# A polysketch attention and routed-experts kernel: shorter float64 conversion, expert work from chunk 1 of batch 0 on, P's stores on one queue, VectorE's part of the evacuations one step later

## The chip, the cores and the metric

The kernel runs on one core of one Trainium2 chip. A core has five engines that run their own instruction queues and meet at semaphores: TensorE (PE: matmuls out of SBUF into PSUM, with weight loads, PEld, beside them), VectorE (DVE), ScalarE (ACT), GpSimd (POOL) and SyncE (SP, which here issues the DMAs). The metric is device microseconds of one execution, the median of several. The profile is of one execution of its own; its span runs from the first to the last instruction of the program.

## The reference

Two blocks in a row, all float32 but for S1 and S2, which arrive as float64.

```python
# attention: B, H, S, D = 4, 4, 1088, 32; r = 8
phi(x) = outer(S1 @ x, S2 @ x)            # 64 features of each row
kv = sum_s phi(k)[s] * v[s];  z = sum_s phi(k)[s]
attn = phi(q) @ kv / (phi(q) . z + 1e-6)
x = attn as rows of (B*S, H*D) = (4352, 128)
# routing: E = 8 experts, F = 1024
P = exp(x @ w_gate - max)
for _ in range(8):
    P /= P.sum(1) + 1e-9;  P /= P.sum(0) + 1e-9;  P *= N / E
out = sum_e P[:, e] * (relu(x @ w1[e]) @ w2[e])
```

So the experts' matrix products need x alone; only their weighting needs P, and P needs the logits of all 4352 rows.

## The kernel before, in words

**Attention.** Each batch goes in three chunks of columns (384, 352 and 352 of 1088). Per batch, `transpose_k` and `transpose_q` turn k and q on VectorE (L247, L249, L241), `keys_ab` projects the keys on TensorE (L260, L264) and ScalarE copies the result to `ab` (L262, L265), `keys_products` multiplies the features on VectorE in three parts (`kp`, L276), and `keys_sums` sums them over the rows on TensorE (L291) and copies the four blocks of the result to `kvz`, by turns on ScalarE (L302) and VectorE (L300). Per chunk, `query_products` (L316, with ScalarE's copies `qa` at L321), `multiply` (VectorE, L328), `fractions` (TensorE, numerator and denominator, L338) and `divide` (VectorE, L350 to L357, writes the columns of `xT`) follow each other. The chunks' query products need four PSUM banks: those of batch 0 are the four banks in which the experts' sums lie later, those of the other batches come from the pool `aps` of four, which the fractions, the key work and the experts' first products share.

**Expert work.** The rows are cut into five pairs of tiles, one pair of 256 columns each and four of 480 each. Six items of expert work (expert 0 on each of the five pairs, expert 1 on pair 1) need no P: they are "plain", their results are kept and weighted at the end. The other 34 items multiply x by a row of P first (`xe`, on GpSimd, L530). An item has four quads, and a quad `k` has four steps `c`. In a step, `first(k, c)` makes a hidden block (L676) and ScalarE takes its ReLU (L680); `combine(k - 1)` makes sums and differences of hidden blocks on VectorE, in step 0 one instruction (L686) and in step 1 two (L688, L689); `second` makes up to two of the seven products (L725) of the quad two before (`LAG = 2`), which are gathered in four PSUM banks. So the seven products per quad stand for eight, and the parts of the result have to be put together afterwards.

**Evacuation.** When the last quad of a group of items has been multiplied, `part(g, k)` takes one of its four banks per step: ScalarE copies (L609, L610, L618, L622 to L624, L629) and VectorE additions. `add_now` (L560) puts an addition at once in VectorE's queue, behind the copies it waits for; `add` (L557) puts it in the list `later`, from which one is taken per step.

**Order.** `steps()` is a generator of these steps, and `fill(n)` takes n units from it, where a step of a 480-column pair is one unit and one of the 256-column pair 256/480. The attention functions are called in an order written out by hand with `fill` between them; `manual_schedule` keeps that order on the engines named, and the other engines' order is made by a scheduler. For batch 0 VectorE, TensorE and ScalarE are ordered by hand, from batch 1 on VectorE and TensorE. Before the change the first `fill(1)` stands after the multiplication of batch 0's last chunk. The generator `attention(b)` yields twelve times per batch, and `counts` has the units between. `routing()` follows: the logits of the three chunks (L363), their transposes (L372) and maximum, the exponential on ScalarE (L448), and eight iterations, each with row sums, scaling and column sums on VectorE (`cs`, L454 to L460), a small matmul that adds the columns up (L464), and the scaling by columns (L467, L470). Between an iteration's `cs` and its matmul stand 3.75 units of expert work. Then `lgT` is turned (L474) and P is stored to DRAM as `pT`, a quarter per batch, by turns from the SyncE and the ScalarE queue (L476); GpSimd's first `xe` reads it back through a DMA. `fill(7)` follows, and the rest of the steps after it.

**Start.** S1 and S2 come as pairs of 32-bit words, and `f64_to_f32` (L33 to L50) makes float32 of them with 16 VectorE instructions on 128x64; L207 turns the result, and `wd` and `wq` are made of it. 17 matmuls on ones (L118) run meanwhile on TensorE.

Of the kernel before, what the change touches and what calls it, by code (L numbers as in the profile page):

```python
# [10 lines left out]
F32 = mybir.dt.float32  # L11
U32 = mybir.dt.uint32
Act = mybir.ActivationFunctionType
Alu = mybir.AluOpType
# [4 lines left out]
def f64_to_f32(nc, pool, raw, shape):  # L19


    p, n = shape
    low, high = raw[:, 0::2], raw[:, 1::2]

    def u32(name):
        return pool.tile([p, n], U32, name=name)

    def f32(name):
        return pool.tile([p, n], F32, name=name)

    mant, tail, top, expo, rest = u32("mant"), u32("tail"), u32("top"), u32("expo"), u32("rest")
    out, ef, inside, over = f32("s12"), f32("ef"), f32("inside"), f32("over")
    nc.vector.tensor_scalar(mant, high, 3, 0x3FFFFFF8, op0=Alu.logical_shift_left, op1=Alu.bitwise_and)  # L33
    nc.vector.tensor_scalar(tail, low, 29, None, op0=Alu.logical_shift_right)
    nc.vector.tensor_scalar(top, high, 0xC0000000, None, op0=Alu.bitwise_and)
    nc.vector.tensor_scalar(rest, low, 0x1FFFFFFF, None, op0=Alu.bitwise_and)
    nc.vector.tensor_tensor(mant, mant, tail, op=Alu.bitwise_or)
    nc.vector.tensor_scalar(expo, high, 20, 0x7FF, op0=Alu.logical_shift_right, op1=Alu.bitwise_and)
    nc.vector.tensor_copy(out, rest)
    nc.vector.tensor_tensor(mant, mant, top, op=Alu.bitwise_or)  # L40
    nc.vector.tensor_copy(ef, expo)

    nc.vector.tensor_scalar(top, mant, 0xFF800000, None, op0=Alu.bitwise_and)

    nc.vector.tensor_scalar(inside, ef, 896.5, None, op0=Alu.is_ge)
    nc.vector.tensor_scalar(over, ef, 1150.5, 3e38, op0=Alu.is_ge, op1=Alu.mult)
    nc.vector.scalar_tensor_tensor(out, out, 2.0 ** -52, top.bitcast(F32), op0=Alu.mult, op1=Alu.mult)
    nc.vector.tensor_tensor(inside, inside, over, op=Alu.add)
# [6 lines left out]
def kernel(  # L55
# [12 lines left out]
    nc = tc.nc  # L68
# [45 lines left out]
    ones = consts.tile([P, P], F32, name="ones")  # L114
    nc.gpsimd.memset(ones, 1.0)
    warm = aps.tile([P, 512], F32, tag="a", name="a")
    for _ in range(17):
        nc.tensor.matmul(warm[:, 0:P], ones, ones, start=True, stop=True)  # L118
    own = consts.tile([P, H], F32, name="own")
    nc.gpsimd.memset(own, 0.0)  # L120
# [27 lines left out]
    loaded = {}  # L148
# [86 lines left out]

        return bank() if b else mps.tile([P, 512], F32, tag=f"s{i}", name="s")

    def transpose_q(b):
        qx = loaded[b][1]
        qT = wk.tile([P, S], F32, tag="qT", name="qT")  # L240
        nc.vector.transpose(out=qT, in_=qx.rearrange("p a d -> p (a d)"))  # L241
        queries[b] = qT

    def transpose_k(b):
        kx = loaded[b][0]
# [35 lines left out]
    def keys_sums(b):  # L281

        kp, vx = products.pop(b), loaded[b][2]
        pv = bank()[:, 0:128].rearrange("p (i c d) -> p i c d", i=2, c=2)
        slots = (slice(0, 3, 2), slice(1, 3), slice(2, 4), slice(2, 5, 2))

        for t in range(NT + 1):
            n = P if t < NT else 64
            for h in range(H):
                i, s = divmod(h, 2)  # L290
                nc.tensor.matmul(pv[64 * s:64 * (s + 1), i], kp[0:n, H * t + h].rearrange("p i j -> p (i j)"),  # L291
                                 vx[0:n, slots[h], t, :], start=(t == 0 and i == 0), stop=(t == NT and i == 1),
                                 tile_position=(0, 64 * s))

        kvz = summed[b % 2]
        for i in range(2):
            for s in range(2):
                sl = slice(64 * s, 64 * (s + 1))
                if s:
                    nc.vector.tensor_copy(kvz[sl, :, i, s, :], pv[sl, i])  # L300
                else:
                    nc.scalar.copy(kvz[sl, :, i, s, :], pv[sl, i])  # L302
        keys[b] = kvz
# [70 lines left out]
    def attention(b):  # L374


        follows = b + 1 < B
        query_products(b, 0)
        yield
        keys_sums(b)  # L380
        if b + 2 < B:
            load_kq(b + 2)
            load_v(b + 2)
        multiply(b, 0)
        if follows:
            transpose_k(b + 1)
        yield
        fractions(b, 0)
        yield
        divide(b, 0)  # L390
        if follows:
            keys_ab(b + 1)
        yield
        query_products(b, 1)
        yield
        multiply(b, 1)
        if follows:
            transpose_q(b + 1)
        yield
        fractions(b, 1)  # L400
        yield
        divide(b, 1)
        if follows:
            keys_products(b + 1, 0)
        yield
        query_products(b, 2)
        yield
        multiply(b, 2)
        if follows:
# [19 lines left out]
    def routing():  # L429
# [70 lines left out]
    later = []  # L500

    def prepare_w(j):
        if j == 0:
# [42 lines left out]
    def part(g, k):  # L546
# [7 lines left out]
        def tile_(tag, pool=keep, bufs=1, width=NMAX):  # L554
            return pool.tile([P, width], F32, tag=tag, name=tag, bufs=bufs)[:, 0:n]

        def add(out, a, b):  # L557
            later.append(lambda: nc.vector.tensor_tensor(out, a, b, op=Alu.add))  # L558

        def add_now(out, a, b):  # L560
            nc.vector.tensor_tensor(out, a, b, op=Alu.add)  # L561

        def put(t):
            y = (y1, y2)[t]
# [69 lines left out]
        if all(own.get(x) for x in (0, 2, 3)) and "v" not in own:  # L634
            own["v"] = True
            add_now(w[upper], own["p7"][upper], own["r"][upper])
            add(z, z, w)
            add(y2, z, f)
            if weighted:
                later.append(lambda: put(1))  # L640
        if all(own.get(x) for x in range(4)):
            add(y1[upper], z[upper], m[upper])
            if weighted:
                later.append(lambda: put(0))

    ends = (nc.scalar, nc.sync, nc.gpsimd, nc.scalar), (nc.sync, nc.scalar, nc.gpsimd, nc.sync)

# [85 lines left out]
    def steps():  # L733

        combined = iter(())
        for k in range(len(quads) + LAG):
# [17 lines left out]
            for c in range(4):  # L754
                if k < len(quads):
                    first(k, c)
                if c == 0 and 0 < k <= len(quads):
                    combined = combine(k - 1)
                next(combined, None)
                for p in todo[2 * c:2 * c + 2]:  # L760
                    second(*p)
                share = pair(groups[items[quads[min(k, len(quads) - 1)][0]][0]][0])[1] / NMAX
                if k >= len(quads):
                    while later:
                        later.pop(0)()
                elif later and (c % 2 or share > 0.9):
                    later.pop(0)()
                yield share
# [50 lines left out]
    with tc.manual_schedule(engines={engines.DVE, engines.PE}):  # L819
# [41 lines left out]
```

## Time and profile before

The median is 964.56 us (3 runs, 964.4 to 964.95). The profiled execution has a span of 962.4 us.

| what | before |
|---|---|
| TensorE busy | 945.7 us, 98% of the span |
| VectorE busy | 559.8 us, 58% |
| ScalarE busy | 393.8 us, 41% |
| GpSimd busy | 121.9 us, 13% |
| granted TensorE clock | 0.997 |
| L676, first expert products | 2560 instructions |
| L725, second expert products | 2240 instructions |
| DMA | 82.34 MB, mean 86 GB/s |

How to read it: a float32 matmul of the program stands as two instructions, and matmuls overlap, so a busy TensorE is not one that works at its full pace. The pace is better read from the number of instructions that start in a stretch. VectorE's share of 58% is a mean of two different stages: in the first 200 us, with the attention and the routing, it is 69 to 95% busy in most stretches of 10 us, and afterwards about 50%. A wait of VectorE or ScalarE matters only where TensorE comes to wait for its result.

### The profile page before, as it was taken

What the parts mean: (1) busy time and instruction counts of PE and PEld (TensorE: products, weight loads), DVE (VectorE), ACT (ScalarE), POOL (GpSimd) and SP (SyncE); (2) the same over time, 40 slices, a digit from 0 to 9 for tenths busy, and PEclk for the clock granted to TensorE, in tenths of its full rate; (3) what the DMA queues carried; (4) which work ended last, traced back from release to release, by engine and by line L of the source; (5) the groups of instructions that cost most, each with busy time, mean ns of one, the idle gap of its engine ahead of it and who ended that gap; (6) DMA issues with size and microseconds to landing.
All of it is one profiled execution on the core that took longest, in us unless ns stands there. A gap on an engine that the chain in (4) does not pass through costs nothing.

```text
span 962.4 us, 13494 instructions
## 1 busy us (share of the span) xinstructions
PE 945.7 (98%) x5510; PEld 393.4 (41%) x5510; DVE 559.8 (58%) x767; ACT 393.8 (41%) x754; POOL 121.9 (13%) x105
## 2 busy tenths in 40 slices
PE   8999999999999999999999999999999999999996
PEld 6644434333333333433333333333333333346664
DVE  7777669875555556844445644444574444447555
ACT  2344344454333334433334433333443333345443
POOL 1000000040222222300002000000200000011100
PEclk9999999999999999999999999999999999999998
DMA  6500000132222222522222422222242222236430
GB/s 191 180 23 1 2 1 1 47 124 62 86 86 84 86 85 96 135 86 85 87 85 95 119 87 86 86 86 86 88 126 86 87 77 78 77 89 167 148 111 12
DMA packets 75405, 82.34 MB, mean 86 GB/s; under 512 B 22416, under 2 KB 60304, under 8 KB 75344
## 3 DMA queue, kind: packets, MB, share of 16 engines
q1 hardware_dynamic: 74288, 81.22, 27.7%
q8 instruction: 43, 0.70, 0.3%
q10 hardware_dynamic: 992, 0.20, 0.1%
q0 software_dynamic: 64, 0.07, 0.1%
q14 instruction: 18, 0.15, 0.0%
HBM read 75.44 MB, written 6.04 MB: 85 GB/s over the span
## 4 chain that ended last, share of the span: by engine, by line
PE 85%; DVE 3%; ACT 1%; issue 0%; POOL 0%; POOLq 0%; DVEq 0%; ACTq 0%
PE a L676 44%; PE s L725 39%; PE a L338 0%; DVE t L686 0%; PE a L316 0%; DVE t L689 0%; DVE cs L460 0%; DVE t L688 0%; DVE y L558 0%; DVE w L561 0%; PE a L291 0%; DVE z L561 0%; PE a L363 0%; DVE rs L454 0%; DVE z L558 0%
## 5 line engine op out<-in xcount | busy, mean ns | idle before, releaser
L676 PE MATMUL a<-xe,w 128*64 128x480 f32 (+1 forms) x2176 | 629.8, 528 | 0.0
L680 ACT ACTIVATE h<-a 128x480 f32<-128x480 f32 (+1 forms) x640 | 341.3, 534 | 517.7 <-PE a L676 505.0
L725 PE MATMUL s<-t,ws 128*64 128x480 f32 (+1 forms) x960 | 416.6, 529 | 0.4 <-DVE t L688 0.3
L686 DVE TENSOR_TENSOR t<-h 128x960 f32<-128x960 f32 (+1 forms) x160 | 215.7, 1349 | 344.4 <-ACT h L680 344.4
L676 PEld LDWEIGHTS a<-xe,w 128*64 128x64 f32 x2176 | 226.8, 137 | 239.6 <-issue 222.4
L725 PE MATMUL s<-h,w 128*64 128x480 f32 (+1 forms) x640 | 286.0, 529 | 0.0
L725 PEld LDWEIGHTS s<-t,ws 128*64 128x64 f32 x960 | 130.5, 137 | 136.2 <-issue 121.0
L725 PE MATMUL s<-t,w 128*64 128x480 f32 (+1 forms) x320 | 143.0, 529 | 0.1
L725 PE MATMUL s<-h,ws 128*64 128x480 f32 (+1 forms) x320 | 143.0, 529 | 0.0
L530 POOL TENSOR_TENSOR xe<-xT,pb 128x960 f32<-128x960 f32 (+1 forms) x33 | 67.1, 2034 | 534.5 <-PE a L676 430.0
L676 PE MATMUL a<-xT,w 128*64 128x480 f32 (+1 forms) x384 | 107.8, 541 | 0.4 <-ACT qa L321 0.3
L689 DVE TENSOR_TENSOR t<-h,t 128x480 f32<-128x480 f32 (+1 forms) x160 | 104.9, 656 | 5.3
L688 DVE TENSOR_TENSOR t<-h,t 128x480 f32<-128x480 f32 (+1 forms) x160 | 104.2, 652 | 4.8
L725 PEld LDWEIGHTS s<-h,w 128*64 128x64 f32 x640 | 87.2, 137 | 43.3 <-issue 40.7
L725 PEld LDWEIGHTS s<-t,w 128*64 128x64 f32 x320 | 43.6, 137 | 49.8 <-issue 29.0
L725 PEld LDWEIGHTS s<-h,ws 128*64 128x64 f32 x320 | 43.7, 137 | 20.6 <-issue 19.7
L676 PEld LDWEIGHTS a<-xT,w 128*64 128x64 f32 x384 | 35.2, 136 | 34.2 <-issue 21.9
L187 POOL TENSOR_TENSOR ws<-w 128x256 f32<-128x256 f32 x8 | 5.8, 727 | 241.5 <-DMA w<-in_moe_w_dram 207.0
L338 PE MATMUL a<-qa,kvz 128*64 128x352 f32 (+1 forms) x96 | 21.1, 474 | 1.5 <-DVE qa L328 1.3
L541 POOL TENSOR_TENSOR y<-y,pb 128x480 f32<-128x480 f32 (+1 forms) x12 | 17.9, 1512 | 22.8 <-DMA pb<-pT 22.8
L316 PE MATMUL a<-qT,wq 64*128 64x352 f32 (+1 forms) x72 | 14.1, 493 | 0.4 <-ACT h L680 0.4
L338 PEld LDWEIGHTS a<-qa,kvz 128*64 128x64 f32 x96 | 9.0, 136 | 10.1 <-issue 5.1
(119 smaller groups left out, 297.4 us busy)
## 6 DMA issues: line engine op xcount, KB each, us to landing
w<-in_moe_w_dram SPq DMA_DIRECT2D x70, 512.0 KB, 3.9
ws<-ws SPq DMA_DIRECT2D x34, 512.0 KB, 3.5
pb<-pT SPq DMA_DIRECT2D x32, 480.0 KB, 3.7
kx<-in_k_dram SPq DMA_DIRECT2D x4, 544.0 KB, 3.8
qx<-in_q_dram SPq DMA_DIRECT2D x4, 544.0 KB, 5.1
v<-in_v_dram SPq DMA_DIRECT2D x32, 64.0 KB, 4.1
pb<-pT SPq DMA_DIRECT2D x8, 256.0 KB, 4.0
out_dram<-yt SPq DMA_DIRECT2D x20, 60.0 KB, 1.9
```

The source lines that it names most:

```text
L187: nc.gpsimd.tensor_tensor(ws[:, 0], a21, a22, op=Alu.add)
L316: nc.tensor.matmul(banks[i][m][:, 0:n], wqf[sl, m, :], qT[sl, lo:hi], start=True, stop=True, tile_position=(64 * i, 0))
L338: nc.tensor.matmul(t[64 * i:64 * (i + 1), 0:n], kvz[:, (i + m) % 2, i].rearrange("p h d -> p (h d)"), ph[i][0][:, 0:n], start=True, stop=T ...
L530: nc.gpsimd.tensor_tensor(xe, xT[:, lo:lo + 2 * n], pb, op=Alu.mult)
L541: nc.gpsimd.tensor_tensor(y, y, pb[:, t * n:(t + 1) * n], op=Alu.mult)
L676: nc.tensor.matmul(ph[sl], loaded_w[j][0][:, P * f + H2 * s:P * f + H2 * (s + 1)], sources[j][:, t * n:(t + 1) * n], start=True, stop=True ...
L680: nc.scalar.activation(out=h[:, c], in_=ph, func=Act.Relu)
L686: nc.vector.tensor_tensor(ts[:, 0:2], h[:, 1::2], h[:, 0:2], op=Alu.subtract)
L688: nc.vector.tensor_tensor(ts[:, 2], h[:, 3], ts[:, 0], op=Alu.subtract)
L689: nc.vector.tensor_tensor(ts[:, 3], h[:, 2], ts[:, 2], op=Alu.subtract)
L725: nc.tensor.matmul(sums[g][i][H2 * s:H2 * (s + 1)], w, x, start=is_first, stop=is_last, tile_position=(0, H2 * s))
```

## The change

It has five parts.

1. `f64_to_f32` has 11 VectorE instructions instead of 16: bit operations are joined in pairs, and the two conversions of integers to float32 are left to the instructions that use them.
2. 15 warm-up matmuls instead of 17.
3. The opening is written in another order. q of batch 0 is transposed in two pieces, the first of 384 columns; the copies of the key sums are a function of their own, `keys_kept`, and the multiplication of the first chunk stands ahead of them. The first `fill(1)` stands directly behind `divide(0, 1)`, and ScalarE's order is written by hand only up to there. The start of batch 1 (its keys, its first query products, its multiplication, the transposes of batch 2's keys) is interleaved with eight `fill(1)` by hand; `attention(1)` begins at its `divide(1, 0)`. `counts` has one unit at nearly every yield, so that 42.25 units of expert work stand before the routing and not 43.25, and `fill(8)` after it instead of `fill(7)`.
4. All four stores of P are issued by SyncE, in the order of batches 1, 2, 0, 3: the first weighted group of rows lies in batches 1 and 2.
5. VectorE's additions of an evacuation go into a list `soon`, which is emptied in the next step, after that step's `combine`; the additions of the list `later` pass through `soon` first. The very last group keeps its additions at once.

It is meant to let TensorE begin expert work earlier and to keep VectorE from standing at the head of its queue behind ScalarE's copies.

```diff
@@ f64_to_f32
-    nc.vector.tensor_scalar(mant, high, 3, 0x3FFFFFF8, op0=Alu.logical_shift_left, op1=Alu.bitwise_and)
-    nc.vector.tensor_scalar(tail, low, 29, None, op0=Alu.logical_shift_right)
...
-    nc.vector.tensor_copy(ef, expo)
...
+    nc.vector.tensor_scalar(mant, high, 3, 0x3FFFFFF8, op0=shift_left, op1=Alu.bitwise_and)
+    nc.vector.tensor_scalar(expo, high, 20, 0x7FF, op0=shift_right, op1=Alu.bitwise_and)
+    nc.vector.scalar_tensor_tensor(mant, low, 29, mant, op0=shift_right, op1=Alu.bitwise_or)
+    nc.vector.tensor_scalar(rest, low, 0x1FFFFFFF, None, op0=Alu.bitwise_and)
+    nc.vector.scalar_tensor_tensor(mant, high, 0xC0000000, mant, op0=Alu.bitwise_and, op1=Alu.bitwise_or)
+    nc.vector.tensor_scalar(over, expo, 1150.5, 3e38, op0=Alu.is_ge, op1=Alu.mult)
     nc.vector.tensor_scalar(top, mant, 0xFF800000, None, op0=Alu.bitwise_and)
+    nc.vector.scalar_tensor_tensor(inside, expo, 896.5, over, op0=Alu.is_ge, op1=Alu.add)
+    nc.vector.scalar_tensor_tensor(out, rest, 2.0 ** -52, top.bitcast(F32), op0=Alu.mult, op1=Alu.mult)
     nc.vector.tensor_tensor(out, out, mant.bitcast(F32), op=Alu.add)
     nc.vector.tensor_tensor(out, out, inside, op=Alu.mult)
@@ the warm-up
-    for _ in range(17):
+    for _ in range(15):
@@ keys_sums
+        sums_of[b] = pv
+
+    sums_of = {}
+
+    def keys_kept(b):
+        pv = sums_of.pop(b)
@@ attention
-        query_products(b, 0)
-        yield
-        keys_sums(b)
+        if b > 1:
+            query_products(b, 0)
+            yield
+            keys_sums(b)
+            multiply(b, 0)
+            if follows:
+                transpose_k(b + 1)
+            yield
+            keys_kept(b)
+            fractions(b, 0)
+            yield
+        divide(b, 0)
         if b + 2 < B:
             load_kq(b + 2)
             load_v(b + 2)
-        multiply(b, 0)
-        if follows:
-            transpose_k(b + 1)
-        yield
-        fractions(b, 0)
-        yield
-        divide(b, 0)
@@ routing
-        for b in range(B):
-            (nc.sync, nc.scalar)[b % 2].dma_start(out=pT[:, b * S:(b + 1) * S],
+        for b in (1, 2, 0, 3):
+            nc.sync.dma_start(out=pT[:, b * S:(b + 1) * S],
@@ part
+        def at_leisure(do):
+            soon.append(lambda: later.append(do))
+
         def add(out, a, b):
-            later.append(lambda: nc.vector.tensor_tensor(out, a, b, op=Alu.add))
+            at_leisure(lambda: nc.vector.tensor_tensor(out, a, b, op=Alu.add))
 
         def add_now(out, a, b):
-            nc.vector.tensor_tensor(out, a, b, op=Alu.add)
+            if end:
+                nc.vector.tensor_tensor(out, a, b, op=Alu.add)
+            else:
+                soon.append(lambda: nc.vector.tensor_tensor(out, a, b, op=Alu.add))
@@ steps
                 next(combined, None)
+                while soon:
+                    soon.pop(0)()
@@ the order
-        transpose_q(0)
+        transpose_q(0, 0, chunks[0][1])
         query_products(0, 0)
         for part_ in range(3):
             keys_products(0, part_)
         keys_sums(0)
         multiply(0, 0)
-        transpose_k(1)
+        transpose_q(0, chunks[0][1])
+        keys_kept(0)
         query_products(0, 1)
         fractions(0, 0)
+        multiply(0, 1)
         divide(0, 0)
-        keys_ab(1)
-        multiply(0, 1)
         fractions(0, 1)
         query_products(0, 2)
         divide(0, 1)
+    with tc.manual_schedule(engines={engines.DVE, engines.PE}):
+        fill(1)
         multiply(0, 2)
+        fractions(0, 2)
         fill(1)
-        fractions(0, 2)
+        transpose_k(1)
         divide(0, 2)
+        keys_ab(1)
+        fill(1)
         transpose_q(1)
-        for part_ in range(3):
-            fill(1)
-            keys_products(1, part_)
-    load_kq(2)
-    load_v(2)
-    counts = {1: (1, 1, 1, 1, 1, 1, 1, 2, 1, 1, 1, 2), 2: (1, 1, 1, 1, 1, 1, 1, 2, 1, 1, 1, 2),
-              3: (1,) * 11 + (0.25,)}
+        load_kq(2)
+        load_v(2)
+        fill(1)
+        keys_products(1, 0)
+        query_products(1, 0)
+        fill(1)
+        keys_products(1, 1)
+        multiply(1, 0)
+        fill(1)
+        keys_products(1, 2)
+        keys_sums(1)
+        transpose_k(2)
+        fill(1)
+        keys_kept(1)
+        fractions(1, 0)
+        fill(1)
+    counts = {1: (1, 1, 1, 1, 1, 1, 1, 1, 1), 2: (1, 1, 1, 1, 1, 1, 1, 1, 1, 1, 1, 2),
+              3: (1, 1, 1, 1, 1, 1, 1, 1, 1, 1, 1, 1.25)}
-        fill(7)
+        fill(8)
```

More of the change, by code (lines that the diff above doesn't have):

```diff
@@ L29, in f32 @@
         return pool.tile([p, n], F32, name=name)
-    mant, tail, top, expo, rest = u32("mant"), u32("tail"), u32("top"), u32("expo"), u32("rest")
-    out, ef, inside, over = f32("s12"), f32("ef"), f32("inside"), f32("over")
-    nc.vector.tensor_scalar(mant, high, 3, 0x3FFFFFF8, op0=Alu.logical_shift_left, op1=Alu.bitwise_and)
-    nc.vector.tensor_scalar(tail, low, 29, None, op0=Alu.logical_shift_right)
-    nc.vector.tensor_scalar(top, high, 0xC0000000, None, op0=Alu.bitwise_and)
-    nc.vector.tensor_scalar(rest, low, 0x1FFFFFFF, None, op0=Alu.bitwise_and)
[L37 to L40, printed above, removed]
-    nc.vector.tensor_copy(ef, expo)
+    mant, top, expo, rest = u32("mant"), u32("top"), u32("expo"), u32("rest")
+    out, inside, over = f32("s12"), f32("inside"), f32("over")
+    shift_right, shift_left = Alu.logical_shift_right, Alu.logical_shift_left
+    nc.vector.tensor_scalar(mant, high, 3, 0x3FFFFFF8, op0=shift_left, op1=Alu.bitwise_and)
+    nc.vector.tensor_scalar(expo, high, 20, 0x7FF, op0=shift_right, op1=Alu.bitwise_and)
+    nc.vector.scalar_tensor_tensor(mant, low, 29, mant, op0=shift_right, op1=Alu.bitwise_or)
+    nc.vector.tensor_scalar(rest, low, 0x1FFFFFFF, None, op0=Alu.bitwise_and)
+    nc.vector.scalar_tensor_tensor(mant, high, 0xC0000000, mant, op0=Alu.bitwise_and, op1=Alu.bitwise_or)
+    nc.vector.tensor_scalar(over, expo, 1150.5, 3e38, op0=Alu.is_ge, op1=Alu.mult)
     nc.vector.tensor_scalar(top, mant, 0xFF800000, None, op0=Alu.bitwise_and)
[L45 to L48, printed above, removed]
+    nc.vector.scalar_tensor_tensor(inside, expo, 896.5, over, op0=Alu.is_ge, op1=Alu.add)
+    nc.vector.scalar_tensor_tensor(out, rest, 2.0 ** -52, top.bitcast(F32), op0=Alu.mult, op1=Alu.mult)
     nc.vector.tensor_tensor(out, out, mant.bitcast(F32), op=Alu.add)
@@ L236, in products_bank, with transpose_q @@
         return bank() if b else mps.tile([P, 512], F32, tag=f"s{i}", name="s")
[L238 to L242, printed above, removed]
+    def transpose_q(b, lo=0, hi=S):
+        if not lo:
+            queries[b] = wk.tile([P, S], F32, tag="qT", name="qT")
+        nc.vector.transpose(out=queries[b][:, lo:hi], in_=loaded[b][1].rearrange("p a d -> p (a d)")[:, lo:hi])
     def transpose_k(b):
@@ L499 @@
     loaded_w, sources, sums, kept, parts, done = {}, {}, {}, {}, {}, {}
-    later = []
+    soon, later = [], []
     def prepare_w(j):
@@ L639, in part @@
             if weighted:
-                later.append(lambda: put(1))
+                at_leisure(lambda: put(1))
         if all(own.get(x) for x in range(4)):
@@ L643, in part @@
             if weighted:
-                later.append(lambda: put(0))
+                at_leisure(lambda: put(0))
     ends = (nc.scalar, nc.sync, nc.gpsimd, nc.scalar), (nc.sync, nc.scalar, nc.gpsimd, nc.sync)
@@ L806 @@
         divide(0, 1)
+    counts = {1: (1, 1, 1, 1, 1, 1, 1, 1, 1), 2: (1, 1, 1, 1, 1, 1, 1, 1, 1, 1, 1, 2),
+              3: (1, 1, 1, 1, 1, 1, 1, 1, 1, 1, 1, 1.25)}
+    with tc.manual_schedule(engines={engines.DVE, engines.PE}):
+        fill(1)
         multiply(0, 2)
+        fractions(0, 2)
         fill(1)
-        fractions(0, 2)
+        transpose_k(1)
         divide(0, 2)
+        keys_ab(1)
+        fill(1)
         transpose_q(1)
-        for part_ in range(3):
-            fill(1)
-            keys_products(1, part_)
-    load_kq(2)
-    load_v(2)
-    counts = {1: (1, 1, 1, 1, 1, 1, 1, 2, 1, 1, 1, 2), 2: (1, 1, 1, 1, 1, 1, 1, 2, 1, 1, 1, 2),
-              3: (1,) * 11 + (0.25,)}
-    with tc.manual_schedule(engines={engines.DVE, engines.PE}):
+        load_kq(2)
[14 more added lines that the diff above has]
+        fill(1)
         for b in range(1, B):
```

## The prediction

> **What bounds the kernel now.** I read the busy time by stage first, then TensorE's waits, then VectorE's waits and its instructions in order of time, each for the stretch in which TensorE falls short. By stage:
>
> ```profile
> 130.00:140.00 10.00, 9.85 (x49) 3.16 (x46) 5.22 (x12) 7.35 (x14) 0.00 (x0) 1.00 0.00 0
> 140.00:150.00 10.00, 7.51 (x42) 3.44 (x42) 9.36 (x18) 2.66 (x5) 0.00 (x0) 1.00 0.01 2
> ...
> 300.00:350.00 50.00, 50.00 (x252) 17.93 (x250) 25.14 (x25) 19.09 (x34) 12.83 (x11) 1.00 0.26 84
> 900.00:940.00 40.00, 40.00 (x374) 26.61 (x372) 21.66 (x39) 18.86 (x50) 2.68 (x3) 1.00 0.39 124
> ```
>
> From about 200 us on TensorE runs without a gap: 50 us hold 250 to 252 matmul instructions of 480 columns, 0.200 us each, and 40 us hold 374 of 256 columns, 0.107 us each. That is the yardstick. Expert work is 2560 (L676) + 2240 (L725) = 4800 instructions, 960 of them 256 wide: 3840 x 0.200 + 960 x 0.107 = 870.7 us. The others at their own pace, from the chain of work: 12 fractions at 1.2, 12 query products at 1.3, 4 key sums at 2.25, 4 key projections at 1.1, logits 2.0, small ones 0.9: about 46 us. The first real matmul starts at 7.32 and the last ends near 954.1, 946.8 us, so some 30 us are lost between them, nearly all before 200 us. Between 130 and 200 the same view, by line, counts 173 of L676 and 151 of L725: 324 x 0.200 = 64.8 of 70 us, 5.2 lost. Who is waited for, over the whole span:
>
> ```profile
> PE a L464 <- DVE cs L460: 2.5, 2, 1.3
> PE a L338 <- DVE qa L328: 1.3, 1, 1.3
> PE a L118 <- POOL own L120: 1.0, 1, 1.0
> PE s L316 <- DVE qa L328: 0.8, 1, 0.8
> PE s L316 <- DVE qT L241: 0.6, 1, 0.6
> ```
>
> It is VectorE: in the opening (L338, L316) and in the routing (L464). These waits are short of the truth, as ends of matmuls are modelled; starts are better. VectorE's opening, in order of time:
>
> ```profile
> 5.54 0.24 DVE L207 STREAM_TRANSPOSE st<-s 128x64 f32<-128x64 f32 x1
> 6.03 1.24 DVE L247 STREAM_TRANSPOSE kT<-kx 128x1024 f32<-128x1024 f32 x1
> 7.82 1.31 DVE L241 STREAM_TRANSPOSE qT<-qx 128x1088 f32<-128x1088 f32 x1
> 9.14 2.69 DVE L276 TENSOR_TENSOR kp<-ab 128x1024 f32<-128x1024 f32 x3
> 13.42 0.23 DVE L300 COPY kvz<-a 64x64 f32<-64x64 f32 x1 [1.60 <-ACT kvz L302]
> 14.16 1.02 DVE L328 TENSOR_TENSOR qa<-qa,s 128x384 f32<-128x384 f32 x2
> ```
>
> VectorE is without a gap until it stands 1.60 us at the copies of the key sums, with the multiplication behind it, which needs nothing of them. And at the routing:
>
> ```profile
> 132.77 0.66 DVE L561 TENSOR_TENSOR z<-s,z 128x480 f32<-128x480 f32 x1 [3.91 <-ACT z L610]
> 133.34 1.44 DVE L372 STREAM_TRANSPOSE lgp<-a 128x384 f32<-128x384 f32 x3
> ...
> 141.11 0.65 DVE L460 TENSOR_REDUCE cs<-p 128x8 f32<-128x280 f32 x1
> ...
> 149.01 0.65 DVE L460 TENSOR_REDUCE cs<-p 128x8 f32<-128x280 f32 x1
> ```
>
> The logits' matmuls are over by 129.8; their transposes L372 stand behind one addition of an evacuation, which waits for ScalarE's copies, until 133.3. So the first column sums come at 141.8 where TensorE is ready at 139.9, and the next at 149.7 where it is ready at 148.0. TensorE's starts show four holes here, of 1.9 (139.60), 1.7 (147.68), 0.5 (166.3) and 0.9 us (172.2): 5.0.
>
> **What the Trainium skill says.** "TensorE: Matmul & The Clock Gate" (Architectural detail: the array is 16x 32x32, not 1x 128x128) has ScalarE and VectorE as strict first-in first-out queues; the rows at 132.77 and 133.34 agree. "VectorE: DVE Perf Modes" (The TRN2 errata) has a fixed cost per instruction, so that small ones are mostly fixed cost; here 64 columns last 0.19 to 0.22 us, 480 columns 0.65. "DMA: Bandwidth & Descriptors" (Issuing engines are not separate DMA queues) says that a second issuing engine saves only issue time; here two of P's stores hold ScalarE's queue 0.89 us and SyncE's 0.67.
>
> **The change part by part.**
>
> *Conversion, 16 to 11 VectorE instructions.* Now it starts at 3.43 and L207 at 5.54: 2.11 us. In the timeline independent ones start 0.10 to 0.14 apart, dependent ones 0.26. With the new order the starts are 3.43, 3.53, 3.68, 3.82, 3.94, 4.08, 4.20, 4.33, 4.47, 4.73, 4.99, and L207 at 5.25, since the three last still wait for one another: 0.3 saved. kx is issued at 1.49 and takes 3.8, so it is there at 5.3, before the new start of its transpose, 5.74. First matmul 7.03. The two warm-up matmuls taken away save nothing and cost nothing: 34 instructions fill 1.00 to 6.91, so 30 end near 6.5.
>
> *Opening.* With 0.3 less in front, qT's first 384 columns (0.58, as L350) are there at 8.1 and the query products start at 8.25 instead of 9.18. kp waits for ScalarE's ab (8.8), is done at 11.55, its sums at 12.6. The multiplication no longer waits for them: 11.5 to 12.45; rest of qT to 13.3; copies to 14.05, in the shadow of the second query products (13.3 to 14.7); fractions 14.7 to 15.95 (now 16.02 to 17.3). divide(0,0) ends at 17.9, divide(0,1) at 20.1 (2.2 each, rows L350 to L357; now 19.3 and 23.3). Expert step one starts at 18.5 instead of 22.9; step two needs divide(0,1) and stands until 20.15. Behind it VectorE is full: multiply 1.0, kT 1.4, divide 2.2, three L686 to L689 1.5, qT 1.3 end at 27.4; TensorE, through step eight at 25.6, stands 1.8 there (products of batch 1 now at 28.64). After that: key sums 31.3 to 33.6, fractions of batch 1 35.25, expert steps through the fourteenth (quad 3, step 2) at 38.1. Now that state is reached at 42.3, less 1.0 for the projections of batch 2, which lie before it now and after it then: 41.3. So 3.2 saved, conversion in it; I take 2.7, as this hand-packed order has some eight hand-overs with no slack and one costs about 0.06 (3.35 to 3.43 after a landing).
>
> *Attention of batches 1 to 3.* The same matmuls and VectorE work; 42.25 units of expert work before routing instead of 43.25, the unit comes after it (8 for 7). VectorE per batch: transposes 2.7, kp 2.8, multiply 2.9, divide 6.7, copies 0.5, 13 steps of expert work 13/4 x 2.65 = 8.6, an evacuation about 3.2: 27.4 us against TensorE's 13 x 1.51 + 10.6 = 30.2. Tight, hidden. Cost 0, between -2 and +2.
>
> *Additions one step later.* They cost nothing, they stand behind the next step's L688/L689 or L686. Counting steps, the evacuation of the third group now falls around the logits: before, its first part comes between logits and L372; then, after L372. So L372 and the maximum run at once, 2 us after the logits, hidden by three expert steps (4.5 us); the exponential and the first column sums follow 4.8 us after the maximum's matmul, against three steps, 4.5: hole 0.3 instead of 1.9. VectorE in iteration 0 then has 3.1 us of expert work instead of 5.0 (141.79 to 146.76), plus 2.95 for the iteration itself: 6.0 against four steps, 6.0: no hole instead of 1.7. By the same sums iteration 2 has 0.7 and iteration 6 0.2: 1.2 for 5.0, 3.8 saved (2.5 to 4.5). After 200 us VectorE has slack: 0.
>
> *P's stores on SyncE.* ScalarE's copy L623 waits 0.82 behind the two issues at 190.66, and TensorE has a hole of 0.46 at 191.6: 0.4 saved. Four issues on SyncE, about 1.3 us, delay the first weights, wanted some ten us later: 0.
>
> Sum: 2.7 + 0 + 3.8 + 0.4 = 6.9; 964.56 - 6.9 = 957.7. The 8.3 us after the last matmul stay.
>
> **Rivals.** (a) *Half of it*: VectorE falls behind in batches 1 and 2 (margin 2.8 us a batch) and 2 us come back per batch, less 0.5 of savings: -6.9 + 3.4 = 961. For: VectorE 27.4 of 30.2. Against: today's 14 steps give 28.1 of 31.7 and TensorE hardly waits. (b) *Slower*: the ScalarE order, no longer written by hand from batch 0's last chunk on, lets every query product wait for banks as at 96.57, where eight instructions take 2.28 instead of 1.45: nine x 0.83 = 7.5 lost, opening not gained, routing 3.8 gained: 968.3. Against: from batch 1 on ScalarE is free in the kernel before too, and only one of nine shows it. (c) *More*: 1.6 us lost around 95 to 100 behind the second evacuation and 0.8 at 390 to 400 and 868 to 874 vanish too, and the opening gives all 3.2: 964.56 - 9.8 = 954.8.
>
> **How the numbers follow.** Forecast 0.60, (a) 0.20, (b) 0.07, (c) 0.13. The range, 954.5 to 962.5, holds the forecast with its bounds (opening 1.5 to 3.2, routing 2.5 to 4.5, middle -2 to +2), (c), and most of (a). Within 0.2% is 962.6 to 966.5: the tail of (a), 0.06. Slower 0.07. Faster 0.87.
>
> **What would show it.** First L260 near 7.0; first L676 near 18.5 and the second step near 20.2; L338 of batch 1 near 35; L372 within 0.5 us of the logits' end, with no L561 ahead of it; L464's wait for cs under 1 us in sum; no pT issue on ScalarE. Wrong if L316 or L338 of batches 1 to 3 wait for ScalarE, or if holes of 1.5 us remain at L464.

## The result, and the profile after

The kernel after takes 956.27 us (median of 4 runs, 955.92 to 956.88) against 964.48 us before in the same comparison: a ratio of 0.9916, 95% interval 0.9899 to 0.9933. It is 8.2 us faster; 6.9 were forecast, and the time lies in the range. One later execution of the kernel after, at a mean granted clock of 0.65, took 1422 us and is left out of every comparison.

The last matmul starts at 945.80 instead of 953.73 in the two profiles, 7.9 us earlier, and what follows it stays (span less end of the last matmul: 8.3 us before, 8.1 after). So all of it was won on TensorE. To say where, I sum in each stage what TensorE's starts lie apart beyond the pace of the matmuls (0.200 us for 480 columns, others in proportion). Each column is one execution; such sums can differ by 0.7 us in a stage between two executions of one kernel, as an experiment below shows:

| stage, ending where TensorE starts | lost before | lost after | won | forecast |
|---|---|---|---|---|
| first L260 (L255 after) | at 7.32 | at 7.35 | 0.0 | in the next |
| first fractions of batch 1 | 8.35 | 6.86 | 1.5 | 2.7 |
| logits | 9.46 | 7.84 | 1.6 | 0 |
| first weighted product | 6.86 | 2.16 | 4.7 | 4.2 |
| last matmul | 6.85 | 6.71 | 0.1 | 0 |

The busy time by stage of the kernel after (columns as before: stretch, its length, then busy time and instructions of TensorE, its weight loads, VectorE, ScalarE and GpSimd, granted clock, DMA share, GB/s):

```profile
130.00:140.00 10.00, 9.02 (x52) 3.56 (x50) 8.59 (x18) 6.54 (x13) 0.00 (x0) 1.00 0.01 2
140.00:150.00 10.00, 10.00 (x59) 6.47 (x57) 9.65 (x18) 3.98 (x7) 0.00 (x0) 1.00 0.00 0
```

From 140 to 150 TensorE has no idle time, where 2.49 us of ten were idle before, and yet VectorE is slightly busier there than before. What TensorE waits for in the kernel after, whole span (total, times, longest):

```profile
PE a L317 <- DVE qT L237: 1.3, 1, 1.3
PE a L114 <- POOL own L116: 1.0, 1, 1.0
PE s L735 <- DVE y L571: 1.0, 1, 1.0
PE a L686 <- DVE xT L358: 0.9, 1, 0.9
PE s L317 <- DVE qT L237: 0.6, 1, 0.6
```

The 2.5 us at the column sums and the waits for `qa` are gone. New are the third line, a product that waits for an addition of an evacuation, and the fourth, the second expert step, which waits for the `xT` of `divide(0, 1)`, as forecast. VectorE's opening after, in order of time:

```profile
4.99 0.24 DVE L203 STREAM_TRANSPOSE st<-s 128x64 f32<-128x64 f32 x1
7.39 0.58 DVE L237 STREAM_TRANSPOSE qT<-qx 128x384 f32<-128x384 f32 x1
9.17 2.69 DVE L271 TENSOR_TENSOR kp<-ab 128x1024 f32<-128x1024 f32 x3 [1.20 <-ACT ab L257]
11.78 1.00 DVE L329 TENSOR_TENSOR qa<-qa,s 128x384 f32<-128x384 f32 x2
13.64 0.23 DVE L301 COPY kvz<-a 64x64 f32<-64x64 f32 x1
```

The multiplication L329 runs ahead of the copies L301, and they follow with no wait; but `kp` starts at 9.17, where it started at 9.14 before. And at the routing:

```profile
124.40 1.73 DVE L373 STREAM_TRANSPOSE lgp<-a 128x384 f32<-128x384 f32 x3 [2.46 <-PE a L364]
...
130.07 0.66 DVE L571 TENSOR_TENSOR z<-s,z 128x480 f32<-128x480 f32 x1 [0.40 <-ACT z L620]
130.76 0.29 DVE L448 TENSOR_REDUCE mx<-a 128x1 f32<-128x128 f32 x1
...
133.70 0.65 DVE L463 TENSOR_REDUCE cs<-p 128x8 f32<-128x280 f32 x1
134.27 0.64 DVE L571 TENSOR_TENSOR y<-s,m 64x480 f32<-64x480 f32 x1
...
139.63 0.66 DVE L463 TENSOR_REDUCE cs<-p 128x8 f32<-128x280 f32 x1
```

The logits' transposes wait for the logits (L364, from 123.48) and for nothing else; the addition `z` comes six us later and waits 0.40 where it waited 3.91. The maximum over the rows (L448) follows `z` at once, 6.4 us after the transposes began.

### The profile page after: what moved, and what is told of

It reads as the page before. It is cut to its first block, busy times and chain, and to the rows that moved or that the text cites. A ratio compares the mean times of both kernels' runs of the same rounds, so it can differ in the third digit from the quotient of the medians.

```text
span 954.3 us, 13484 instructions
## 1 busy us (share of the span) xinstructions
PE 940.5 (99%) x5506; PEld 459.1 (48%) x5506; DVE 561.1 (59%) x763; ACT 393.7 (41%) x754; POOL 124.2 (13%) x105
## 4 chain that ended last, share of the span: by engine, by line
PE 95%; DVE 3%; ACT 1%; issue 0%; POOL 0%; DVEq 0%; POOLq 0%; ACTq 0%
PE a L686 48%; PE s L735 42%; PE a L317 1%; PE a L339 1%; PE a L286 1%; PE a L114 1%; PE a L255 0%; DVE kp L271 0%; DVE t L699 0%; DVE qa L329 0%; DVE qT L237 0%; ACT h L690 0%; DVE t L696 0%; PE a L364 0%; DVE t L698 0%
## 5 line engine op out<-in xcount | busy, mean ns | idle before, releaser
L686 PE MATMUL a<-xe,w 128*64 128x480 f32 (+1 forms) x2176 | 636.9, 528 | 0.0
L696 DVE TENSOR_TENSOR t<-h 128x960 f32<-128x960 f32 (+1 forms) x160 | 213.8, 1337 | 346.3 <-ACT h L690 346.2
L686 PEld LDWEIGHTS a<-xe,w 128*64 128x64 f32 x2176 | 242.9, 137 | 208.0 <-issue 158.9
L686 PE MATMUL a<-xT,w 128*64 128x480 f32 (+1 forms) x384 | 112.7, 540 | 1.0 <-DVE xT L358 0.9
L686 PEld LDWEIGHTS a<-xT,w 128*64 128x64 f32 x384 | 37.8, 137 | 31.6 <-issue 18.9
L531 POOL TENSOR_TENSOR xe<-xT,pb 128x480 f32<-128x480 f32 x2 | 3.1, 1578 | 139.2 <-DVE w L571 139.2
```

The lines of the kernel that those rows point to most:

```text
L686: nc.tensor.matmul(ph[sl], loaded_w[j][0][:, P * f + H2 * s:P * f + H2 * (s + 1)], sources[j][:, t * n:(t + 1) * n], start=True, stop=True ...
L696: nc.vector.tensor_tensor(ts[:, 0:2], h[:, 1::2], h[:, 0:2], op=Alu.subtract)
```

## The experiments

My theory after the result: VectorE's queue decides, at three places. The additions put off free the routing; the new opening frees the start; and the attention's 1.6 us, not forecast, come from the same additions. The main rival: the new order alone carries the gain, since it also moves the evacuations by a step against the logits. All kernels are compared with the kernel before on the same chip.

**The additions at once again.**

```diff
-            soon.append(lambda: later.append(do))
+            later.append(do)
...
-                soon.append(lambda: nc.vector.tensor_tensor(out, a, b, op=Alu.add))
+                nc.vector.tensor_tensor(out, a, b, op=Alu.add)
```

> The kernel after, with VectorE's additions of an evacuation put at once in its queue again (no list soon). Theory, as in the prediction: the later additions are what frees VectorE at the routing, so most of the 3.8 us come back, about 959.8, with two holes of 1.5 to 2 us in TensorE at the column-sum matmuls. Rival: the new count of units alone does it, since the third group's first part now falls behind the transposes of the logits whether its addition is late or not; then the time stays within 0.7 us of 956.3, and the 1.2 us hole of the kernel after near 134 us, where a product waits for the late addition y, is gone.

965.04 us, ratio 1.0003 (0.9995 to 1.0011): the whole gain is gone, more than twice what the theory said. Stage losses: opening 7.3, attention 14.1, routing 5.3. So the routing gives back 3.1 of the 3.8 expected, but the attention loses 6.2, most of it at one place. VectorE there, TensorE's waits, and the granted clock (the last but two column of the stretches):

```profile
101.77 0.66 DVE L571 TENSOR_TENSOR w<-s,r 64x480 f32<-64x480 f32 x1 [4.88 <-ACT r L639]
102.47 0.66 DVE L565 TENSOR_TENSOR z<-z,w 128x480 f32<-128x480 f32 x1
103.16 0.23 DVE L301 COPY kvz<-a 64x64 f32<-64x64 f32 x1
```

```profile
PE a L339 <- DVE kvz L301: 2.7, 2, 2.4
PE a L467 <- DVE cs L463: 1.4, 1, 1.4
```

```profile
100.00:102.00 2.00, 1.15 (x4) 0.14 (x1) 0.23 (x1) 1.12 (x2) 0.00 (x0) 1.00 0.00 0
102.00:104.00 2.00, 0.47 (x2) 0.35 (x3) 1.63 (x5) 0.21 (x1) 0.00 (x0) 0.87 0.00 0
104.00:106.00 2.00, 2.00 (x8) 1.37 (x8) 1.97 (x3) 0.00 (x0) 0.00 (x0) 0.50 0.00 0
106.00:108.00 2.00, 2.00 (x11) 1.34 (x9) 1.79 (x6) 0.21 (x1) 0.00 (x0) 0.78 0.00 0
```

In the new order the last part of the second evacuation falls between batch 3's key sums and the copies of their result. Its addition `w` stands 4.88 us for ScalarE's copy, the copies `kvz` stand behind it, and batch 3's fractions behind them. TensorE stands 2.4 us, and then works at half clock. In the kernel after the copies stand ahead of `w`, which comes when ScalarE's copy is done:

```profile
97.63 0.23 DVE L301 COPY kvz<-a 64x64 f32<-64x64 f32 x1 [3.17 <-ACT kvz L303]
...
100.14 0.66 DVE L571 TENSOR_TENSOR w<-s,r 64x480 f32<-64x480 f32 x1
```

In the routing the rival was half right. VectorE in the kernel without the late additions:

```profile
130.90 1.73 DVE L373 STREAM_TRANSPOSE lgp<-a 128x384 f32<-128x384 f32 x3 [2.46 <-PE a L364]
...
136.57 0.66 DVE L571 TENSOR_TENSOR z<-s,z 128x480 f32<-128x480 f32 x1 [1.79 <-ACT z L620]
...
138.97 0.27 DVE L448 TENSOR_REDUCE mx<-a 128x1 f32<-128x128 f32 x1
```

In the new order `z` stands behind the logits' transposes without the list too. What the list still changes is the maximum: here it stands behind `z`, which waits 1.79 us, and another addition, and comes 8.1 us after the transposes began instead of 6.4. TensorE then waits 1.4 us for the first column sums.

**The same, with the copies of the key sums ahead of that part.**

```diff
                 transpose_k(b + 1)
+            keys_kept(b)
             yield
-            keys_kept(b)
             fractions(b, 0)
```

> The kernel after without the list soon, but with the copies of the key sums of batches 2 and 3 one yield earlier, ahead of the fill in which the second evacuation's last part falls. Theory: in the kernel without soon (965.0) the hole of 2.95 us at 100.2, where the fractions of batch 3 wait for those copies behind an addition that waits 4.88 us for ScalarE, and the half clock behind it make 4.3 us of the 8.8: about 960.7, no clock below 1 near 100 us. Rival: the addition stands in front of something else then (the divisions, L696) and TensorE waits there: 963 or more.

961.42 us, ratio 0.9968 (0.9957 to 0.998). The clock stays at 1.00 and TensorE is busy throughout:

```profile
102.00:104.00 2.00, 2.00 (x13) 0.70 (x10) 2.00 (x3) 0.57 (x1) 0.00 (x0) 1.00 0.00 0
104.00:106.00 2.00, 2.00 (x10) 0.80 (x7) 1.76 (x6) 0.79 (x2) 0.00 (x0) 1.00 0.00 0
```

The attention's loss falls from 14.1 to 10.4. So that collision was worth 3.6 to 3.7 us (batch 2's copies, which the edit moves too, included); the additions at once cost 2.6 more in the attention and 3.1 in the routing.

**The new order alone**, with the old conversion, 17 warm-up matmuls, additions at once and P's stores on two queues: the diff's other parts undone, the conversion by its old lines.

```diff
-    for _ in range(15):
+    for _ in range(17):
...
-        for b in (1, 2, 0, 3):
-            nc.sync.dma_start(out=pT[:, b * S:(b + 1) * S],
+        for b in range(B):
+            (nc.sync, nc.scalar)[b % 2].dma_start(out=pT[:, b * S:(b + 1) * S],
...
-            soon.append(lambda: later.append(do))
+            later.append(do)
...
-                soon.append(lambda: nc.vector.tensor_tensor(out, a, b, op=Alu.add))
+                nc.vector.tensor_tensor(out, a, b, op=Alu.add)
```

> The kernel before with the new hand-written order, the split of the key sums' copies and the new counts alone: old conversion, 17 warm-up matmuls, additions at once, P's stores on two queues. Theory: the opening (1.3 us by the two traces) and the attention (1.8 us) alone, 961.4. Rival, the order and the count of units carry the routing's gain too: 957.0.

965.42 us, ratio 1.0008 (1.0000 to 1.0016). Neither expectation: opening 7.0, attention 14.3, routing 5.9. The order does win 1.4 in the opening and 1.0 in the routing, where it alone puts `z` behind the transposes, and loses 4.9 in the attention, most of it at the same collision (`w` waits 4.89 us): alone it is worth nothing, and the gain is not carried by it alone.

**The additions alone**, in the old order.

```diff
+            soon.append(lambda: later.append(do))
...
-            later.append(lambda: nc.vector.tensor_tensor(out, a, b, op=Alu.add))
+            at_leisure(lambda: nc.vector.tensor_tensor(out, a, b, op=Alu.add))
...
-            nc.vector.tensor_tensor(out, a, b, op=Alu.add)
+            if end:
+                nc.vector.tensor_tensor(out, a, b, op=Alu.add)
+            else:
+                soon.append(lambda: nc.vector.tensor_tensor(out, a, b, op=Alu.add))
...
                 next(combined, None)
+                while soon:
+                    soon.pop(0)()
```

> The kernel before, with the list soon alone. Theory: the addition that stood ahead of the logits' transposes moves behind them, so the routing gains 3 to 4 us and the attention stages up to 1: about 960.5. Rival, that the gain of the change lies in the new order of opening and units: under 1 us, 963.5 or more.

962.36 us, ratio 0.9976 (0.9967 to 0.9986), half of the expected gain, all of it in the routing (6.86 to 4.34); the attention stays at 9.5. From TensorE's list of waits:

```profile
PE a L683 <- POOL xe L528: 0.8, 2, 0.5
PE s L732 <- DVE y L568: 0.5, 1, 0.5
PE a L464 <- DVE cs L460: 0.5, 1, 0.5
```

The column sums' wait shrinks from 2.5 to 0.5 as foreseen; `z` stands behind the transposes here too and waits 0.61. Two others take part of it back: the first weighted products now wait for GpSimd, for which SyncE loads P only from 195.96, behind a DMA of `ws` in its queue (before at 196.56, in the kernel after from 182.85), and a product waits for a late addition. By the medians the two parts alone give 2.0 and -1.1 us, together, with the small edits, 8.2.

**The old conversion and 17 warm-ups.** The diff's first two parts undone, in short:

```diff
-    nc.vector.scalar_tensor_tensor(mant, low, 29, mant, op0=shift_right, op1=Alu.bitwise_or)
+    nc.vector.tensor_scalar(tail, low, 29, None, op0=Alu.logical_shift_right)
+    nc.vector.tensor_tensor(mant, mant, tail, op=Alu.bitwise_or)
...
-    for _ in range(15):
+    for _ in range(17):
```

> The kernel after with the old conversion of 16 instructions and 17 warm-up matmuls. Theory of the prediction: 0.3 us slower, 956.6, first L260 later by 0.3. Rival: the start of kp waits for something else (in both traces it starts at 9.14 and 9.17), so the conversion is worth nothing: 956.3 within 0.1.

956.73 us, ratio 0.9916 (0.9903 to 0.993), the ratio of the kernel after. The transpose of `s` (L203 in the kernel after) starts at 5.35 against 4.99, so the conversion is 0.36 us later, and yet the first key projection starts at 7.34 against 7.35. The two profiles can't tell what the conversion is worth: in both the warm-up matmuls end last, at 7.41 and 7.42, and hide it, and the full clock came at 5.96 us in the one and at 6.92 in the other.

**12 warm-ups.**

```diff
-    for _ in range(15):
+    for _ in range(12):
```

> The kernel after with 12 warm-up matmuls instead of 15. Theory: in the profile of after the 30 warm-up instructions ran at half clock until 6.9 us and ended at 7.35, past the keys' transpose (6.95), so the shorter conversion was lost behind them; 24 end at 6.1 even at half clock, the first L255 comes at 7.0 to 7.2 in every run, and the time is 0.1 to 0.3 lower, 956.1. Rival: with fewer warm-ups the clock is granted later still, the key projections and query products run at half clock, and the time is 0.3 to 1 higher.

956.61 us, ratio 0.9921 (0.9907 to 0.9934): no gain. TensorE in order of time from 5.5 us on, after and then with 12:

```profile
5.21 2.21 PE L114 MATMUL a<-ones 128*128 128x128 f32 x11
7.35 0.45 PE L255 MATMUL a<-wd,kT 128*64 128x64 f32 x8
```

```profile
5.22 1.27 PE L114 MATMUL a<-ones 128*128 128x128 f32 x5
6.82 0.98 PE L255 MATMUL a<-wd,kT 128*64 128x64 f32 x26 [0.33 <-DVE kT L242]
```

The first part of the theory holds: in the profile of after the warm-ups end behind the keys' transpose and hide the conversion, and with 12 the first projection comes 0.53 earlier. But batch 1's fractions come only 0.27 earlier, and the last matmul 0.11. The times of one kernel lie 1 us apart, so a worth of 0.1 to 0.3 us of either edit stays open.

**P's stores on two queues again.**

```diff
-        for b in (1, 2, 0, 3):
-            nc.sync.dma_start(out=pT[:, b * S:(b + 1) * S],
+        for b in range(B):
+            (nc.sync, nc.scalar)[b % 2].dma_start(out=pT[:, b * S:(b + 1) * S],
```

> The kernel after with P's stores by turns on SyncE and ScalarE again, in the order of the batches. Theory, as in the prediction: ScalarE stands 0.8 us at the issues and TensorE loses 0.4: 956.7. Rival: ScalarE has slack there, 956.3; or P comes later to the weights and the first weighted product waits for GpSimd, as in the kernel before with the list soon alone (two waits, 0.8 us), then 957 to 958.

956.62 us, ratio 0.9917 (0.9903 to 0.9931). ScalarE in order of time:

```profile
180.78 0.89 ACTq L479 DMA_DIRECT2D pT<-lgT  x2
181.71 0.55 ACT L620 COPY z<-s 64x480 f32<-64x480 f32 x1 [0.79 <-DMA pT<-lgT]
```

The wait is there, 0.79 us. The routing's loss is unchanged (2.15). The stage after it loses 0.6 more, in a hole of 0.65 at 197; that the stores cause this hole is not shown (such a hole comes and goes between executions, as seen below), and the difference in the times, 0.35, is within their scatter.

**The late addition ahead of the row sums.**

```diff
         nc.scalar.activation(out=pw[:, :, 0:E], in_=lg, func=Act.Exp, bias=mx[:, 0:1])
+        while soon:
+            soon.pop(0)()
```

> The kernel after with one edit: the list soon is also emptied in the routing right behind the exponential, so that the addition y stands ahead of the first iteration's row sums, where VectorE waits 0.6 us for ScalarE anyway. Theory: the 1.2 us hole near 134 us (a product that waits for y, whose bank it takes) is the price of the late additions, and goes: 955.3. Rival: the column sums come 0.7 later instead and L467 waits for them: 956.0 to 956.3.

955.52 us, ratio 0.9906 (0.9892 to 0.992). VectorE and, below, TensorE:

```profile
131.18 0.64 DVE L573 TENSOR_TENSOR y<-s,m 64x480 f32<-64x480 f32 x1
131.86 0.30 DVE L456 TENSOR_SCALAR p<-p 128x272 f32<-128x272 f32 x1
```

```profile
PE s L737 <- DVE t L700: 0.8, 2, 0.5
```

`y` fits into VectorE's wait for the exponential; L456 starts at 131.86 where its fellow L454 of after starts at 131.84. The wait for `y` is gone, and part of it comes back as a wait for `t` (a hole of 0.85 at 139.5 against one of 0.43 at 159 after): the routing's loss falls by 0.55. The loss of the last stage rises by 0.6 in this profile, in a hole of 1.0 at 196, which is not shown to be the edit's (see both order edits below). The times say 0.7, within the scatter.

**The opening's order mended.**

```diff
         keys_ab(1)
-        fill(1)
         transpose_q(1)
+        fill(1)
...
-        fill(1)
         keys_kept(1)
+        fill(1)
         fractions(1, 0)
```

> The kernel after with two edits of the order: q of batch 1 is transposed ahead of the fill whose three VectorE instructions (1.5 us) it stood behind, and the copies of batch 1's key sums stand ahead of the fill whose L696 waits 1.56 us for ScalarE. Theory: these two are what the opening lost against the prediction; the holes of 1.44 us at 26.1 and 0.65 at 35.6 shrink to about 0.2 each: 954.8. Rival: VectorE is full in this stretch, so that what is moved ahead only moves the wait to the products of the keys, and the time stays within 0.4 of 956.3.

955.19 us, ratio 0.9901 (0.9887 to 0.9915). VectorE's transpose now runs at 24.54, where it was at 26.28, and TensorE's query products follow at once:

```profile
24.54 1.30 DVE L237 STREAM_TRANSPOSE qT<-qx 128x1088 f32<-128x1088 f32 x1
25.77 0.65 DVE L696 TENSOR_TENSOR t<-h 128x512 f32<-128x512 f32 x1
```

```profile
26.17 1.56 PE L317 MATMUL a<-qT,wq 64*128 64x384 f32 x8
```

Batch 1's fractions start at 34.71 instead of 36.42, and the opening's loss is 5.5 instead of 6.9. The hole at 35.6 is gone too. VectorE had room to have it so: a hole of 0.42 at the key sums is all that comes back.

**Both order edits**, the diffs of the last two experiments together.

> The kernel after with the edits of both the kernel that empties soon behind the exponential (955.5) and the kernel with the new opening order (955.2). Theory: the two holes lie 100 us apart and their gains, 0.8 and 1.2 us, add up: 954.4. Rival: what the one gains in the opening comes back as the wait for t (0.85 us at 139.5) or for the first weighted rows near 196 us, and the time is that of the better of the two, 955.2.

955.13 us, ratio 0.9902 (0.9888 to 0.9915): not the sum. The losses are 5.5, 8.2, 1.4 and 6.8, that is 1.4 and 0.75 won and 0.3 lost. To see whether it beats the kernel after, the two ran beside each other on one chip:

> The kernel after, unchanged, beside the next one on the same chip, since its 956.27 and the 955.1 of the kernel with both order edits were measured on different chips. Theory: 956.3, that is 1.1 us or more above the other. Rival: the 1.1 us is the difference of chips, and both lie within 0.5 us.

> The kernel with both order edits (soon emptied behind the exponential, new opening order), unchanged, beside the kernel after. Theory: the stage losses of its profile, 1.4 us less in the opening and 0.75 less in the routing, 0.3 more in the attention, make it 1.1 to 1.8 us faster than after: 954.5 to 955.2. Rival: within 0.5 us of after.

The kernel after: 956.53 to 957.63 in four runs, ratio 0.9923 (0.991 to 0.9937). With both edits: 954.06 to 955.8 in four runs, ratio 0.9896 (0.9881 to 0.9911). Every run of the second is faster than every one of the first; their medians, 954.7 and 957.1, lie 2.4 us apart. It beats both kernels. A second profile of this same kernel has losses of 5.6, 8.4, 1.6 and 7.5; it has the hole at 196 (0.97 us), which the first does not have. So that hole does not follow from the edits alone, and how much of the gain is the opening's and how much the routing's is known only as far as two profiles tell.

## Why the prediction was right, point by point

*What bounds it.* Right: TensorE's holes before 200 us, each behind VectorE's queue. From the first weighted product on the loss stays as it was (6.85 and 6.71).

*Conversion.* The size was right (0.36 us measured, 0.3 forecast), its way to the end was not. The step "first matmul 7.03" failed because of the sentence that the 30 warm-ups end near 6.5: in this profile they ran at about 0.2 us each and ended at 7.42. That took for granted that the full clock comes at the same time in every run; it came at 4.91 us before and at 6.92 after, and the warm-ups start 0.21 us apart until then and 0.11 from then on. In the five profiles with the new conversion and 15 warm-ups in which it came by 5.1, the first projection starts at 6.92 to 7.16, near the forecast; even then nothing clear reaches the end.

*Opening.* The mechanism was right, the term mis-sized: 1.5 us instead of 2.7. The fractions of batch 1 came at 36.42, 1.2 us late: 0.3 is the first matmul, 0.3 more had gathered when the key sums began (31.86 for 31.3), and the last 0.6 is the failed step, "key sums 31.3 to 33.6, fractions of batch 1 35.25". Between them the order has a fill whose L696 waits 1.56 us for the ReLU of a step that TensorE has only just made, and the copies stand behind it; the forecast has no term for this wait. The allowance for hand-overs, 0.06 us each, was also small by its own example, 3.35 to 3.43. The wait of 1.8 us for batch 1's queries was forecast, and came as 1.3 to 1.4. The kernel with the opening mended removes both and loses 1.4 less in its profile.

*Attention.* Forecast 0, won 1.6, and right for a poor reason: I booked "the same matmuls and VectorE work". In truth two large terms met there. The new order alone loses 4.9 us in this stage, most of it by one addition ahead of the copies of batch 3's key sums, and with the late additions that comes back and 1.6 more. I had listed the late additions as a matter of the routing. But the 1.6 are not theirs alone, as my theory after the result had it. From the last fractions of batch 2 to the first of batch 3, around the second evacuation, 2.4 us are lost before, 2.4 with the list alone, 1.1 after, and 1.1 in the new order without the list but with the copies moved: there the new order wins, once nothing collides. At the first evacuation, from batch 1 to 2, it is 2.0, 2.1, 1.2 and 2.5: there it takes both. Rival (c) named the second evacuation's loss around 95 to 100, and that part of it came true; the holes at 390 to 400 and 866 did not vanish.

*Routing.* Right in the main mechanism and nearly in size: 4.7 won, 4.2 forecast with P's stores. The transposes no longer stand behind `z`, and the column sums' matmul waits no more. But the forecast booked all this on the additions: the order alone also moves `z` behind the transposes. By the profiles the order alone wins 1.0 here, the list alone 2.5, both 4.7. The hole I put at 0.3 there is 1.2 and stands at another instruction: a product takes the PSUM bank that the late addition `y` still reads. I costed the late additions at nothing, and this was their price; with `y` placed elsewhere 0.55 of it was saved. "The Trainium skill", "TensorE: Matmul & The Clock Gate" (Architectural detail: the array is 16x 32x32, not 1x 128x128), on strict first-in first-out queues, is what all of this rests on, and the runs agree: in the new order `z` waits 1.79 us at the head of VectorE's queue without the list and 0.40 with it, and the maximum behind it comes 1.7 us later without. The fall from 3.91 us before is the work of both parts.

*P's stores.* ScalarE's wait is as forecast (0.79 against 0.82); the 0.4 us for TensorE can't be told from 0.

*Rivals.* (a) did not come: the attention lost less than before, not more. (Its sum, -6.9 + 3.4, should have 3.5 by its own terms, which changes nothing.) (b) did not come: no query product of the kernel after waits for ScalarE. That the order alone is as slow as the kernel before shows how near a slower outcome was, by another way than (b).

## What to carry to other kernels

An instruction that waits at the head of a first-in first-out queue costs by what stands behind it, so ask of every wait which of the next instructions lead to the bound engine, and put the waiting one behind them; one addition of an evacuation cost nothing, about 0.5 us or 3.7 us according to its neighbours. Parts of a change that reorders queues should be costed together: here one part alone was worth 2.0 us, the other nothing, and both, with the small edits, 8. A result read later also frees its buffer later, so look for the next writer of that buffer.

## What was not expected of the hardware

A hole of 2.4 to 3 us was enough to cost TensorE its clock. In the kernel without the late additions the shares by stretch are 0.87, 0.50 and 0.78 from 102 to 108; (0.13 + 0.50 + 0.22) x 2 / 0.5 gives 3.4 us at half clock, and the one with the new order alone shows the same again (0.95, 0.50 and 0.70). "TensorE: Matmul & The Clock Gate" (Part 1: The HAM clock gate) speaks of a window of some 3.4 us and of half clock after an idle one; the 3.4 us agree, but the hole was shorter than the window, and no window was idle. In every trace the full clock lasts a whole number of times 3.413 us (here 29 times, then one such window at half clock, then 250 times). Cut into these windows, the profile without the late additions reads:

```profile
100.05:103.47 3.42, 1.10 (x4) 0.14 (x1) 1.55 (x3) 1.17 (x3) 0.00 (x0) 1.00 0.00 0
103.47:106.88 3.41, 3.35 (x10) 2.30 (x12) 3.05 (x7) 0.16 (x1) 0.00 (x0) 0.50 0.00 0
```

TensorE was busy 32% of the window ahead of the half clock, by modelled ends, and 30% in the kernel with the new order alone. In the 13 profiles of this case at full clock, all 15 windows in which it was busy 38% or less were followed by half clock, and none in which it was busy 55% or more; between these no window lies. So where a hole falls in the windows matters beside its length, and that differs between executions. Of 13 executions of the kernel with the new order alone, the five with a mean clock of 0.998 took 964.1 to 964.9 us and the eight with 0.996 or 0.997 took 965.4 to 966.4; that the five escaped the half clock is likely, but none of the five has a trace. In these two profiles a hole of 2.4 us, or near 3 by TensorE's starts, cost an estimated 1.7 us more than it lasted, half of 3.4.
